# Fading the mLSTM state on ScalarE and adding only its diagonal blocks on VectorE

## The chip, the cores and the metric

One core of a Trainium2 chip runs the whole program. The metric is the device time of one execution in microseconds (us). Engines are named as in the profile: PE is TensorE, DVE is VectorE, ACT is ScalarE, POOL is GpSimd, SP is SyncE, whose queue (SPq) issues nearly all DMAs.

## The reference

Three layers follow each other; only the first is touched. It is an mLSTM over 2 batches, 8 heads, 768 time steps and a head width of 40:

```python
for t in range(S):
    m_new = np.maximum(f_gate[:, :, t] + m, i_gate[:, :, t])
    f_stab = np.exp(f_gate[:, :, t] + m - m_new)
    i_stab = np.exp(i_gate[:, :, t] - m_new)
    C = f_stab[..., None, None] * C + i_stab[..., None, None] * np.einsum('bhd,bhe->bhde', vt, kt)
    n = f_stab[..., None] * n + i_stab[..., None] * kt
    y_t = sigmoid(o_gate_t) * einsum('bhde,bhe->bhd', C, qt) / max(|n . qt|, 1)
```

The second layer is a spatially gated MLP, the third a channel mix, both with float32 results.

## The kernel before, in words

The 768 steps of a batch are cut into 6 chunks of 128, so there are 12 positions, taken in the order `SEQ` = 0, 6, 1, 7, 2, 8, ... (a chunk of batch 0, then the same chunk of batch 1). At a position the kernel computes the scores within the chunk (`scores`, `logd`), the contribution of earlier chunks through the state (`inter`), the state after the chunk (`state`, L478), the products with the values (`intra`), and the division (`normalise`), and transposes the result (`turn`) for the MLP.

The state of a batch is a tile `cn` of 120 rows by 8 x 41 columns. Heads go in groups of three (0 to 2, 3 to 5, 6 to 7): one matmul per group (L491) makes the keys of all the group's heads times the values of all of them, so of each 120 x 123 result in the PSUM tile `sp` only the three 40 x 41 blocks on the diagonal, a head with itself, are wanted. For a batch's first chunk ACT copies `sp` to `cn` (L512); for later ones DVE computes `cn * decay + sp` with one instruction for each group (`gather`, L500). In both cases POOL then multiplies `cn` by a 0/1 mask `bm_sb` (`blocks`, L505, two instructions) and clears the blocks off the diagonal. `bm_sb` is made once by ACT (L510) from a loaded tile `bm_raw`. The next reader of `cn` is `inter` (L527) of the same batch, two positions later. The last chunk of a batch makes no state, so there are ten state updates: two first ones and eight later ones.

The order of each engine's queue is fixed when the program is built, by a small planner. It keeps a clock for PE and a free time for DVE (`V`), ACT (`A`) and POOL (`P`). Work off PE is a `chain` of steps, each with an engine and a cost, which becomes ready 0.2 after the clock; a step follows the one before it by its cost plus `HOP` = 0.15. Whenever PE's clock moves (`beat`), `advance` issues the steps whose planned start lies before it, earliest start first; chains of weight splitting (`widen`, `wsp_half`) carry a handicap (`late`). Between the tasks of a position `fill(n, 1.0)` puts up to n matmuls of the MLP (`vp`, `up`) into PE's queue as long as their inputs' planned due time is within 1.0 of the clock. While the plan sees PE waiting with no filler ready, in the first eight positions, `heat` inserts matmuls on the identity (`wp`, L348). A changed cost in a chain can thus change the order in all four queues. `sp` holds one of six PSUM banks of the pool `psa` until the mark `("Cs", i)`.

Of the kernel before, what the change touches and what calls it, by code (L numbers as in the profile page):

```python
# [7 lines left out]
F32 = mybir.dt.float32  # L8
# [3 lines left out]
BF16 = mybir.dt.bfloat16  # L12
AF = mybir.ActivationFunctionType
ALU = mybir.AluOpType
# [3 lines left out]
def tile_mlstm_gmlp_channelmix(  # L18
# [25 lines left out]
    SEQ = [6 * b + c for c in range(6) for b in range(2)]  # L44
    P = 128
    H, D = 8, 40
    DA = D + 1
# [8 lines left out]
    GRP = ((0, 3), (3, 3), (6, 2))  # L56

    vec, act, pool, pe = nc.vector, nc.scalar, nc.gpsimd, nc.tensor
# [5 lines left out]
    at = tc.alloc_tile_pool(name="at", bufs=1, side="right")  # L64
# [88 lines left out]
    def beat(cost):  # L153
        clock[0] += cost
        advance(clock[0])
# [14 lines left out]
    def chain(key, *steps, ready=None):  # L170
        running.append(Chain(key, steps, clock[0] + 0.2 if ready is None else ready, 0.0))

    def finish(*keys, stall=True):
        for k in keys:
            while any(b[0] == k or b[0][0] == k for b in back):
                if not force_feed():
                    break
            for c in [c for c in running if c.has(k)]:
                while c in running and c.has(k):
                    advance(c.start(), skip=c)  # L180
                    if not c.open():
                        finish(split[0], stall=False)
                    if c in running and c.has(k):
                        issue(c)
        if stall:
            at_least(max([done.get(k, 0.0) for k in keys], default=0.0))
# [40 lines left out]
    def bank(pl, tag, name, *keys):  # L227
        own(tag, 6 if tag == "at" else 2, *keys)
        return pl.tile([P, 512], F32, tag=tag, name=name)
# [61 lines left out]
    def rows3(t, w):  # L291
# [8 lines left out]
    ig = gp.tile([16, S], F32, name="ig")  # L300
    f2, i2, ex_sb, pk_sb = (gp.tile([96, n], F32, name=nm)
                            for nm, n in (("f2", P), ("i2", P), ("ex_sb", 120), ("pk_sb", 6 * NCH)))
    bm_sb = at.tile([120, H * DA], BF16, name="bm_sb")
    mg = gp.tile([16, S + 1], F32, name="mg")
    ones = gp.tile([96, P], F32, name="ones")
    dec = at.tile([120, 6, NCH], F32, name="dec")
# [8 lines left out]
    def load_qk(i):  # L315
        b, c = divmod(i, NCH)
        t = at.tile([P, 2, 4, P], F32, tag="qk", name=f"qk{i}", bufs=2)
        for hh in range(2):
            e = load(t[64 * hh:64 * hh + D], qk[b, c, hh], 164)
        st["q", i], st["k", i] = t[:, 0], t[:, 1]  # L320
        st["at", i] = e
# [11 lines left out]
    def load_o(u):  # L333
        b, j = divmod(u, 2)
        o = at.tile([P, 3, DM], F32, tag="og", name=f"og{u}", bufs=3)
        load(o, o_tok[b, j], 480)
        st["o", u] = o
# [13 lines left out]
    for a in 'i f d o2 o0 q'.split():  # L351
        dict(f=lambda: sync.dma_start(out=fg, in_=f_gate), i=lambda: sync.dma_start(out=ig, in_=i_gate),
             d=lambda: sync.dma_start(out=id_sb, in_=ident), o=lambda: load_o(int(a[1])), q=lambda: load_qk(SEQ[0]))[a[0]]()
# [125 lines left out]
    def state(i):  # L479
        b, c = divmod(i, NCH)  # L480
        vt = st["vt", i]
        if c == NCH - 1:
            return
        wait(("kw", i))
        kw = st.pop(("kw", i))
        sp = bank(psa, "at", f"sp{i}", ("Cs", i))
        if c == 0:
            st["C", b] = at.tile([120, H * DA], F32, name=f"cn{b}")
        cn = st["C", b]
        for g, (h0, n) in enumerate(GRP):  # L490
            pe.matmul(sp[:n * D, h0 * DA:(h0 + n) * DA],  # L491
                      kw[:, h0:h0 + n, :].rearrange("p h d -> p (h d)"),
                      vt[:, h0:h0 + n, :].rearrange("p h d -> p (h d)"), start=True, stop=True)
        beat(0.57)
        parts = ((3 * D, slice(0, 6 * DA)), (2 * D, slice(6 * DA, 8 * DA)))

        def gather():
            for g, (h0, n) in enumerate(GRP):
                sl = slice(h0 * DA, (h0 + n) * DA)
                vec.scalar_tensor_tensor(out=cn[:n * D, sl], in0=cn[:n * D, sl], in1=sp[:n * D, sl],  # L500
                                         scalar=dec[:n * D, 3 * b + g, c:c + 1], op0=ALU.mult, op1=ALU.add)

        def blocks(eng, x):
            for n, sl in parts:
                eng.tensor_tensor(out=cn[:n, sl], in0=bm_sb[:n, sl], in1=x[:n, sl], op=ALU.mult)  # L505

        if c == 0:
            def fetch():
                if i == SEQ[0]:
                    act.copy(bm_sb, bm_raw)  # L510
                for n, sl in parts:
                    act.copy(cn[:n, sl], sp[:n, sl])  # L512

            chain(("C", i), ("A", 0.6, fetch, ("Cs", i)), ("P", 1.0, lambda: blocks(pool, cn)))
        else:
            finish(("dec", 0), stall=False)
            chain(("C", i), ("V", 0.75, gather, ("Cs", i)), ("P", 1.0, lambda: blocks(pool, cn)))

    def inter(i):
        b, c = divmod(i, NCH)  # L520
# [230 lines left out]
    def wait(*keys):  # L751
        while True:
            gap = eta(keys) - clock[0]
            if gap <= 0.02:
                break
            if fillers and eta(fillers[0][2]) <= clock[0] + 0.1:
                fill(1)
            elif warm[0] and gap > 0.2:
                heat(1)
                advance(clock[0])  # L760
            else:
                break
        finish(*keys)
# [26 lines left out]
    bm_raw = at.tile([120, H * DA], F32, tag="vr", name="bm_raw", bufs=2)  # L790
# [41 lines left out]
    def position(p):  # L832
# [20 lines left out]
        def st_():  # L853
            if p == 2:
                finish(("eg", "c"), ("dec", 0), stall=False)
                gp.release()
                lsp_.append(tc.alloc_tile_pool(name="lsp", bufs=1, side="left", reuse_waits="tile"))
                vec.tensor_scalar(out=omu_sb, in0=mu_sb, scalar1=-1.0, scalar2=1.0, op0=ALU.mult, op1=ALU.add)
            state(i)
# [64 lines left out]
    while todo:  # L924
        p = todo[0]["p"]
# [185 lines left out]
    for g in range(2 * B):  # L1111
# [8 lines left out]
        for j in range(3):  # L1120
            sl = slice(j * P, (j + 1) * P)
# [6 lines left out]
        for j in range(3):  # L1128
            sl = slice(j * P, (j + 1) * P)
# [120 lines left out]
```

## Time and profile before

| | |
|---|---|
| three runs | 332.76, 334.08, 334.0 us; median 334.0 |
| profiled execution | 334.12 us, span 332.4 us |
| mean granted PE clock | 0.937 of full speed |
| PE busy | 310.5 us (93%) |
| PE weight loads busy | 287.8 us (87%) |
| DVE busy | 230.0 us (69%) |
| ACT busy | 158.2 us (48%) |
| POOL busy | 157.0 us (47%) |

The profile is one execution. A busy time is the union of an engine's instructions; "idle before" names what ended a wait. The granted clock is a share of full speed, and has two levels, 0.5 (1.2 GHz) and 1.0 (2.4 GHz). The mLSTM takes the first 127 us or so of the span, its states the stretch from 20 to 111 us; the matmuls of the MLP's first layer fill PE beside it until 142 us.

### The profile page before, as it was taken

The page shows a single profiled execution, that of the slowest core. Times are in us where ns is not written, and L with a number is a line of the kernel's source. Part 1 is how long each engine was busy: PE and PEld are TensorE (multiplying, and loading weights), DVE is VectorE, ACT ScalarE, POOL GpSimd, SP SyncE. Part 2 cuts the span into 40 slices and gives each one's busy share as a digit, 9 for nine tenths or more (in the row PEclk, how much of TensorE's full clock was granted, in tenths as well). Part 3 has the DMA queues.
Part 4 walks back from the last instruction along what each step waited for, and adds up shares of the span by engine and source line. Part 5 has one row for each costly group of instructions (what it writes and reads, how often), then busy time and mean ns, then how long its engine had stood idle before and what let it go on. Part 6 is the DMA issues. An engine that isn't in the chain of part 4 may idle for free.

```text
span 332.4 us, 5459 instructions
## 1 busy us (share of the span) xinstructions
PE 310.5 (93%) x1985; PEld 287.8 (87%) x1985; DVE 230.0 (69%) x424; ACT 158.2 (48%) x316; POOL 157.0 (47%) x203
## 2 busy tenths in 40 slices
PE   5899996999999999999999999658999999999995
PEld 3586675898988988999999999547999999999995
DVE  6558599976877887776697956996655655654621
ACT  4552363238454344552345426348783753753620
POOL 4046267674878763783384660664501601601600
PEclk9656998799999999999999999965999999999999
DMA  6855651343543322356023320320001001001001
GB/s 182 270 140 173 221 152 63 94 151 100 166 117 100 113 63 65 98 167 210 2 80 127 106 78 14 109 78 0 0 2 60 3 20 39 2 20 41 0 20 41
DMA packets 12854, 28.97 MB, mean 87 GB/s; under 512 B 2099, under 2 KB 6187, under 8 KB 12827
## 3 DMA queue, kind: packets, MB, share of 16 engines
q1 hardware_dynamic: 12795, 28.56, 27.6%
q8 instruction: 16, 0.26, 0.3%
q14 instruction: 11, 0.09, 0.1%
q0 software_dynamic: 32, 0.07, 0.1%
HBM read 26.35 MB, written 1.97 MB: 85 GB/s over the span
## 4 chain that ended last, share of the span: by engine, by line
PE 76%; DVE 12%; ACT 3%; DMA 3%; issue 2%; POOL 2%; SPq 1%; DVEq 0%; POOLq 0%; ACTq 0%
PE spp L614 15%; PE vv L614 13%; PE kp L614 12%; PE vp L614 6%; PE wop L614 6%; PE up L614 5%; PE av L543 5%; PE rp L614 4%; DMA qk<-in_qk_dram 3%; PE sc L444 3%; PE wp L348 2%; PE ld L453 2%; DVE wbits L274 2%; DVE wbits L270 2%; PE sp L491 2%
## 5 line engine op out<-in xcount | busy, mean ns | idle before, releaser
L1103 POOL TENSOR_TENSOR sq<-sq 128x384 f32<-128x384 f32 x32 | 27.1, 852 | 60.9 <-ACT sq L1102 60.9
L614 PE MATMUL kp<-xk,wk 128*128 128x384 f32 x256 | 46.3, 338 | 4.6 <-DVE vs L1001 4.6
L614 PE MATMUL spp<-wsp,vn 128*128 128x384 f32 x288 | 50.4, 334 | 0.0
L614 PEld LDWEIGHTS spp<-wsp,vn 128*128 128x128 f32 x288 | 49.9, 188 | 0.0
L614 PEld LDWEIGHTS kp<-xk,wk 128*128 128x128 f32 x256 | 44.7, 189 | 5.2 <-DVE vs L1001 5.2
L614 PE MATMUL vv<-wv,k 128*128 128x320 f32 x288 | 42.9, 309 | 0.0
L614 PEld LDWEIGHTS vv<-wv,k 128*128 128x128 f32 x288 | 42.4, 188 | 0.0
L232 DVE TENSOR_TENSOR k<-sq,k 128x384 fp32r<-128x384 f32 x32 | 25.6, 801 | 21.7 <-ACT k L1104 21.7
L614 PE MATMUL up<-xg,w_u 128*128 128x256 f32 x192 | 32.5, 295 | 0.9 <-ACT u L696 0.6
L614 PE MATMUL vp<-w_v,xg 128*128 128x512 f32 x96 | 30.0, 428 | 2.0 <-ACT xg L605 1.2
L614 PE MATMUL wop<-gt,wo 128*128 128x384 f32 x128 | 27.4, 375 | 3.5 <-DVE vs L1001 2.5
L614 PEld LDWEIGHTS wop<-gt,wo 128*128 128x128 f32 x128 | 25.8, 216 | 4.9 <-ACT wv L285 3.0
L543 PEld LDWEIGHTS av<-kvq,dt 128*128 128x128 f32 x192 | 27.4, 215 | 0.8
L614 PEld LDWEIGHTS up<-xg,w_u 128*128 128x128 f32 x192 | 26.4, 190 | 1.8 <-ACT u L696 0.8
L1002 POOL TENSOR_TENSOR vs<-vs,u 128x384 f32<-128x384 f32 x16 | 20.5, 1279 | 13.7 <-DVE vs L1001 13.7
L543 PE MATMUL av<-kvq,dt 128*128 128x41 f32 x192 | 26.8, 294 | 0.0
L466 DVE TENSOR_TENSOR dt<-dt,sc 128x512 f32<-128x512 f32 x24 | 16.4, 682 | 11.2 <-ACT dt L463 9.4
L274 DVE SCALAR_TENSOR_TENSOR wbits<-wsq,wbits 128x320 int32<-128x320 int32 (+1 forms) x27 | 20.1, 748 | 4.2 <-ACT wsq L269 3.9
L1102 ACT ACTIVATE sq<-kp 128x384 f32<-128x384 f32 x32 | 15.4, 491 | 15.6 <-PE kp L614 15.6
L614 PEld LDWEIGHTS vp<-w_v,xg 128*128 128x128 f32 x96 | 17.9, 198 | 5.4 <-ACT xg L605 1.9
L463 ACT ACTIVATE dt<-ld 128x512 f32<-128x512 f32 x24 | 14.4, 600 | 17.0 <-PE ld L455 9.2
L1142 DVE TENSOR_TENSOR ob<-rs,vv 128x320 f32<-128x320 f32 x12 | 5.8, 487 | 21.3 <-PE vv L614 21.3
(160 smaller groups left out, 578.9 us busy)
## 6 DMA issues: line engine op xcount, KB each, us to landing
kvq<-in_kvq_dram SPq DMA_DIRECT2D x10, 516.0 KB
qk<-in_qk_dram SPq DMA_DIRECT2D x24, 160.0 KB
wraw<-in_w_k_dram SPq DMA_DIRECT2D x6, 512.0 KB
wraw<-in_w_v_dram SPq DMA_DIRECT2D x8, 320.0 KB
wraw<-in_w_sp_dram SPq DMA_DIRECT2D x12, 192.0 KB
og<-in_o_tok_dram SPq DMA_DIRECT2D x4, 480.0 KB
out_dram<-ob SPq DMA_DIRECT2D x12, 160.0 KB
w_inv<-in_w_in_dram SPq DMA_DIRECT2D x3, 512.0 KB
```

Source lines behind the costliest of these rows:

```text
L232: eng.tensor_tensor(out=out, in0=a, in1=b.bitcast(F32), op=ALU.subtract)
L270: vec.tensor_single_scalar(out=bits, in_=low_, scalar=29, op=ALU.logical_shift_right)
L274: vec.scalar_tensor_tensor(out=t["bits"], in0=t["sq"].bitcast(I32), scalar=3, in1=t["bits"], op0=ALU.logical_shift_left, op1=ALU.bitwise_or)
L348: pe.matmul(wp[:, :256], junk[:, :P], junk, start=True, stop=True)
L444: pe.matmul(st["sc", i, x][:, h * P:(h + 1) * P], k_[64 * x:64 * x + D, h, :], q_[64 * x:64 * x + D, h, :], start=True, stop=True)
L463: ("A", 0.48, lambda: act.activation(out=d2, in_=ld, func=AF.Exp), ("e", i, hh)),
L466: ("V", 0.6, lambda: vec.tensor_tensor(out=d2, in0=d2, in1=sc, op=ALU.mult)))
L543: pe.matmul(av[:, 4 * hh + h, :], A[:, h, :], vt[:, 4 * hh + h, :], start=True, stop=True)
L614: pe.matmul(out[0], l, x, start=j == 0, stop=j == len(prs) - 1)
L1002: ("P", 0.96, lambda: pool.tensor_tensor(out=vs, in0=vs, in1=ut[b][:, d, sl], op=ALU.mult)),
L1102: chain(("k2", g, f), ("A", 0.37, lambda: act.activation(out=sq, in_=ps, func=AF.Relu), ("kp", g, f)), ("P", 0.96, lambda: pool.tensor_ten ...
L1103: ("P", 0.96, lambda: pool.tensor_tensor(out=sq, in0=sq, in1=sq, op=ALU.mult)),
```

## The change

The state starts as zeros (one memset on POOL for each batch). For a later chunk ACT first multiplies `cn` by its decay, one instruction for each of the three groups (`fade`). DVE then adds from `sp` only the blocks on the diagonal (`gather`): instruction j takes the heads j, j+3, j+6 (a stride of three heads) and rows 0 to 40(j+1), and multiplies `sp` by column j of `bm_sb`, which is 1 in the 40 rows of the head and 0 above them. `bm_sb` becomes a tile of 120 x 3, one strided copy on ACT. POOL's multiplication by the mask goes. The planner's chain was DVE 0.75 (ACT 0.6 for a first chunk), then POOL 1.0; it is now ACT 0.75 (0.2 for a first chunk), then DVE 1.0, and the PSUM bank is given back after the DVE step as the second step of the chain, not the first.

```diff
-    bm_sb = at.tile([120, H * DA], BF16, name="bm_sb")
+    bm_sb = at.tile([120, 3], F32, name="bm_sb")
...
-        parts = ((3 * D, slice(0, 6 * DA)), (2 * D, slice(6 * DA, 8 * DA)))
+
+        s3, c3 = (t.rearrange("p (h d) -> p h d", h=H) for t in (sp[:, :H * DA], cn))
+
+        def fade():
+            if i == SEQ[0]:
+                act.copy(bm_sb, bm_raw[:, 0:3 * DA:DA])
+            if c > 0:
+                for g, (h0, n) in enumerate(GRP):
+                    sl = slice(h0 * DA, (h0 + n) * DA)
+                    act.activation(out=cn[:n * D, sl], in_=cn[:n * D, sl], func=AF.Copy, scale=dec[:n * D, 3 * b + g, c:c + 1])
 
         def gather():
-            for g, (h0, n) in enumerate(GRP):
-                sl = slice(h0 * DA, (h0 + n) * DA)
-                vec.scalar_tensor_tensor(out=cn[:n * D, sl], in0=cn[:n * D, sl], in1=sp[:n * D, sl],
-                                         scalar=dec[:n * D, 3 * b + g, c:c + 1], op0=ALU.mult, op1=ALU.add)
-
-        def blocks(eng, x):
-            for n, sl in parts:
-                eng.tensor_tensor(out=cn[:n, sl], in0=bm_sb[:n, sl], in1=x[:n, sl], op=ALU.mult)
+            for j, r in enumerate((D, 2 * D, 3 * D)):
+                vec.scalar_tensor_tensor(out=c3[:r, j:H:3], in0=s3[:r, j:H:3], in1=c3[:r, j:H:3],
+                                         scalar=bm_sb[:r, j:j + 1], op0=ALU.mult, op1=ALU.add)
 
         if c == 0:
-            def fetch():
-                if i == SEQ[0]:
-                    act.copy(bm_sb, bm_raw)
-                for n, sl in parts:
-                    act.copy(cn[:n, sl], sp[:n, sl])
-
-            chain(("C", i), ("A", 0.6, fetch, ("Cs", i)), ("P", 1.0, lambda: blocks(pool, cn)))
+            pool.memset(cn, 0.0)
         else:
             finish(("dec", 0), stall=False)
-            chain(("C", i), ("V", 0.75, gather, ("Cs", i)), ("P", 1.0, lambda: blocks(pool, cn)))
+        chain(("C", i), ("A", 0.75 if c else 0.2, fade), ("V", 1.0, gather, ("Cs", i)))
```

## Rows read from the trace of the kernel before

**Rows 1.** The page's first part: busy time, share and instructions by engine.
```profile
PE 310.5 (93%) x1985; PEld 287.8 (87%) x1985; DVE 230.0 (69%) x424; ACT 158.2 (48%) x316; POOL 157.0 (47%) x203
```
**Rows 2.** Stretches: length, PE, PEld, DVE, ACT, POOL busy, PE clock, DMA share, GB/s.
```profile
40.00:50.00 10.00, 9.21 (x75) 7.43 (x71) 9.67 (x23) 5.64 (x12) 6.77 (x9) 1.00 0.55 176
50.00:60.00 10.00, 7.31 (x36) 5.82 (x33) 9.38 (x19) 3.33 (x6) 8.26 (x11) 0.74 0.19 54
...
201.00:226.00 25.00, 17.25 (x84) 15.22 (x82) 23.15 (x40) 13.70 (x29) 10.49 (x10) 0.85 0.23 67
```
**Rows 3.** PE's waits from 37 to 142 us, the four longest: total, times, longest.
```profile
PE tp L591 <- DVE x L568: 1.5, 3, 0.8
PE vp L614 <- ACT xg L605: 1.2, 1, 1.2
PE tp L591 <- POOL x L571: 0.7, 1, 0.7
PE vp L614 <- DVE xg L232: 0.7, 1, 0.7
```
**Rows 4.** Stretches of 1 us around PE's waits, columns as in rows 2.
```profile
46.00:47.00 1.00, 0.31 (x1) 0.30 (x2) 0.94 (x4) 0.67 (x2) 1.00 (x2) 1.00 0.42 160
...
52.00:53.00 1.00, 0.27 (x2) 0.20 (x2) 1.00 (x3) 0.00 (x0) 0.74 (x2) 1.00 0.47 180
53.00:54.00 1.00, 0.29 (x3) 0.14 (x1) 0.55 (x2) 0.62 (x1) 1.00 (x3) 1.00 0.00 0
54.00:55.00 1.00, 0.53 (x2) 0.19 (x1) 1.00 (x3) 0.30 (x1) 1.00 (x2) 0.94 0.00 0
55.00:56.00 1.00, 0.25 (x1) 0.25 (x2) 1.00 (x4) 1.00 (x3) 1.00 (x2) 0.50 0.00 0
...
61.00:62.00 1.00, 1.00 (x14) 0.93 (x12) 1.00 (x1) 0.00 (x0) 1.00 (x1) 0.65 0.25 87
```
**Rows 5.** Groups by form: count, busy us, mean ns of one, idle before, releaser.
```profile
L505 POOL TENSOR_TENSOR cn<-bm_sb,cn 120x246 f32<-120x246 bf16 x10 | 8.4, 843 | 11.6 <-ACT cn L512 7.0 <-DVE cn L500 4.5
...
L505 POOL TENSOR_TENSOR cn<-bm_sb,cn 80x82 f32<-80x82 bf16 x10 | 4.7, 468 | 0.0
...
L1003 ACT CAST gt<-vs 128x384 fp32r<-128x384 f32 x16 | 8.2, 510 | 12.0 <-POOL vs L1002 12.0
...
L1039 ACT ACTIVATE tm<-x,omu_sb 128x384 f32<-128x384 f32 x24 | 13.9, 610 | 0.0
...
L512 ACT COPY cn<-sp 120x246 f32<-120x246 f32 x2 | 0.7, 365 | 2.7 <-PE sp L491 2.7
...
L384 ACT CAST Lxc<-f 96x128 fp32r<-96x128 f32 x1 | 0.3, 297 | 0.0
...
L500 DVE SCALAR_TENSOR_TENSOR cn<-cn,dec,sp 120x123 f32<-120x123 f32 x16 | 4.7, 334 | 0.0
...
L500 DVE SCALAR_TENSOR_TENSOR cn<-cn,dec,sp 80x82 f32<-80x82 f32 x8 | 2.3, 288 | 0.0
```
**Rows 6.** The tile wp: ns min/median/max, first and last start.
```profile
L348 PE MATMUL wp<-id_sb x61: 269/371/421, 3.6 to 38.9; 128*128 128x256 bf16 x61
```
**Rows 7.** DVE and POOL in order of time: start, us, instruction.
```profile
28.81 1.65 DVE L381 TENSOR_TENSOR i<-i,m 96x128 f32<-96x128 f32 x1
...
41.24 0.42 DVE L270 TENSOR_SCALAR wbits<-w_inu 128x512 int32<-128x512 int32 x1
...
47.08 1.28 POOL L232 TENSOR_TENSOR w_u<-wsq,w_u 128x512 fp32r<-128x512 f32 x1
...
47.59 1.05 DVE L270 TENSOR_SCALAR wbits<-w_inu 128x512 int32<-128x512 int32 x1
```
**Rows 8.** ACT in order of time, with the idle time before.
```profile
43.85 0.48 ACT L605 CAST xg<-tp 128x384 fp32r<-128x384 f32 x1 [0.79 <-PE tp L591]
...
53.22 0.62 ACT L285 CAST w_u<-wsq 128x512 fp32r<-128x512 f32 x1 [2.04 <-DVE wsq L278]
54.70 0.62 ACT L683 CAST vn<-vr 128x512 fp32r<-128x512 f32 x1 [0.86 <-DVE vr L681]
55.23 0.47 ACT L605 CAST xg<-tp 128x384 fp32r<-128x384 f32 x1
```

## The prediction

> **What bounds the kernel now.** I read the busy shares first, then the stretches, then PE's waits, then the queues around the longest of them. PE is busy for 310.5 us of a span of 332.4 [rows 1]. So an edit that touches no matmul can gain only where PE stands still or runs at the lower clock. The stretches say where that is: PE is nearly full everywhere except between 40 and 60 us, where DVE is the full engine (9.67 and 9.38 of 10), and between 201 and 226 us [rows 2]. The second place lies 90 us behind the last state update and is DVE splitting weights; I leave it as it is. The states are updated in the first place and up to 111 us. From 37 to 142 us PE's four longest waits come to 1.5 + 1.2 + 0.7 + 0.7 = 4.1 us [rows 3]. Between 52 and 56 us PE is busy for only 0.27, 0.29, 0.53 and 0.25 us of each microsecond, and behind that the granted clock falls to 0.50, its lower level of 1.2 GHz, and is back in the row of 61 to 62; the single poor microsecond at 46, between full ones, cost no clock [rows 4]. What the fall costs: 0.06 + 6 x 0.5 + 0.35 = 3.4 us of full-speed time, less the half of the 0.75 us in which PE stood idle anyway at 55, makes 3.0 us [rows 4]. So 4.1 us of waits and 3.0 us of clock are all that the change can win near its own place, and the same mechanism is what it can lose.
>
> **The change part by part.**
>
> *POOL* loses 8.4 + 4.7 = 13.1 us in 20 instructions [rows 5]. It gains two memsets; the trace has none of their shape, so each costs between nothing and the 0.843 of the removed instruction of like size, and they lie where POOL now waits 7.0 us for ACT's first copies [rows 5]. None of PE's long waits is for the mask's output: what releases them is a transposition's input or `xg` [rows 3]. So the 13.1 us are worth nothing directly. Indirectly they could free DVE, which waits for POOL in places: the same DVE instruction takes 0.42 us at 41.24 and 1.05 at 47.59, while POOL's 1.28 us subtraction runs [rows 7]. I compared each DVE instruction beside the ten masks with its undisturbed twin: about 1.9 us are lost in all, most of it in one of 1.65 us at 28.81 [rows 7], none of it in front of a wait in [rows 3]. I take nothing, with 0 and -1.9 us as the ends.
>
> The Trainium skill (SBUF — State Buffer, section "SBUF: two separate sides") says VectorE and GpSimd lock one shared port pair for whole instructions, and that a VectorE instruction with two SBUF inputs is among those that block. By it every removed mask could free DVE for its whole length, at most 13.1 us as an estimate, and the sum would be that much lower. The 1.05 us at 47.59 agrees that such blocking exists; the 1.9 us found beside the masks says that these rarely collide.
>
> *ACT* gains eight fades. The trace shows no such instruction. A cast of 96x128 takes 297 ns; a scale taken from a tile costs 610 - 510 = 100 ns more at 128x384 [rows 5]. So 0.40 us for 123 columns, about 0.36 for 82; together 1.16, or about 0.96 in a row, since neighbours overlap by 0.1. The ends are 3 x 0.297 = 0.9 and 3 x 0.61 = 1.8 us. It loses the two copies at first chunks (0.365 and a smaller one) and most of one cast. A fade reads only `cn` and the decays, not the new matmul, so it can run while PE still makes `sp`. ACT has the room: it is busy 5.64 and 3.33 us of the two tight stretches [rows 2], and stands idle 0.79 us at 43, just about one fade, and 2.04 us before 53.22 [rows 8]. Cost nothing, as long as it goes into those gaps. Without them, it stands before the next cast of `xg` with its whole 0.96 us (the slower rival below).
>
> *DVE* keeps three instructions per state, of the same widths: 2 x 0.334 + 0.288 = 0.96 us in place of the same sum [rows 5]. The strided heads are not in the trace; the ends are no change and double. I take no change, since a mean of 334 ns for 123 columns is mostly fixed cost. New are the gathers of the two first chunks, 2 x 0.96 = 1.9 us, between 19 and 29 us, where PE is at the half clock and its queue carries the `wp` matmuls, 61 by 38.9 us [rows 6]; the next real dependence there is on DMA, so nothing. By the costs in the chains the first chunk's gather delays DVE's plan by 1.0 and lightens POOL's by as much, which about cancels in the due time that decides the number of `wp`; the ends are -7 and +7 of them, at 0.1 to 0.2 us, within +-1.4 us.
>
> *PE* and *DMA* get no new work. SP's queue keeps its order, and the mask's load stays. The bank of `sp` is held up to one fade longer; no wait of PE in [rows 3] is for a bank, so nothing, and 0.96 us if that were wrong at one place.
>
> *The order.* This is where I expect the effect. A gather becomes ready 0.75 + 0.15 later in the plan than before and is costed 0.25 higher. So weight splitting and score products that stood behind it on DVE go ahead of it. At the state at 45 us this lets the split that feeds `w_u` start one gather, about 0.8 us, earlier; POOL's 1.28 us at 47.08 then ends before the DVE instruction at 47.59, which gets back its 1.05 - 0.42 = 0.6 us [rows 7]. I take 0.5 for the two transposition waits behind it. At the state at 54.6 us the low half of `xg` gets a later due time (0.25 to 1.15 by the costs). In PE's queue a single `vp` matmul is put there as a filler ahead of eight `av`, and PE waits 1.2 us for the `xg` cast of 55.23 with the `av` ready behind it [rows 3, 8]. A filler must be due within 1.0; with the later due time it drops behind the `av`, and the 1.2 us goes. What is late next is then that same `xg` with the `av` already done, some tenths.
>
> *Sum.* -0.5 - 1.2 = -1.7 us on the profiled 334.12 us (span 332.4 and 1.7 around it), which lies 0.1 above the median of 334.0. I predict 332.3 us.
>
> **The rivals.**
>
> *The clock stays up.* If those 1.7 us of work move into the poor microseconds 52 to 56, PE's clock may not fall there: another -3.0, 329.3 us. For it: the one poor microsecond at 46 did not bring the clock down. Against: two waits of 0.7 for the transposition remain in the same place.
>
> *Nothing moves.* The plan slides but PE's queue keeps its order, or what is won at 52 to 56 is waited for again at the next `xg`: 334.0, give or take 0.5.
>
> *Slower: a fade in front of `xg`.* ACT runs in order. At 54.70 to 55.7 it casts `vn` and directly behind it `xg`, for which PE waits [rows 8]. If the plan puts the fade of 0.96 us between the two, PE's wait grows by that; it decides from the point where a fade starts after the `vn` cast rather than in the 2.04 us before 53.22. The gather then waits too, and behind it on DVE the score product and the low half of `xg`: 0.96 + 0.96 for two steps in a row. With one such place 334.0 + 1.9 = 335.9, and if the longer gap keeps the clock down half as long again or lowers it at a second place (1.5 to 3.0 us), up to 338.9. I give 336.5. For it: DVE is the full engine there [rows 2], so every wait of a gather is passed on. Against: the fade is ready early, since it waits only for the `inter` matmuls before it.
>
> *It does not do what it says.* Should the strided gather cost double, DVE gets 0.96 us more at each of ten states, two of them in the tight stretch: +1.9 us, in with the slower case.
>
> **How the numbers follow.** The forecast 0.36, with its own range 331.3 to 333.3; clock up 0.24; nothing moves 0.18; slower 0.22. About 0.5% of 334, 1.7 us, is what a measurement of this kernel tells from no change, and the three runs shown lie 1.3 us apart. The forecast sits on that bound, so half of it and all of the clock case make faster: 0.18 + 0.24 = 0.42, and 0.02 from runs below in the case where nothing moves. Slower is 0.22, same the remaining 0.34. The range reaches from the middle of the clock case's spread, 328.8, to just past the middle of the slower one, 336.8.
>
> **What would show it.** Right: L505 gone, three ACT instructions of 0.35 to 0.40 us in ACT's gaps, three DVE instructions at the old length; PE's wait of 1.2 us on `xg` gone and fewer poor microseconds between 52 and 56; the stretches behind 142 us as long as before. The clock rival: no row at 0.50 between 54 and 62. Wrong: a fade between `vn` and `xg` casts, longer gathers, other numbers of `wp`, or a difference that arises behind 201 us, for which I have made no case.

## The result and the profile after

| | before | after |
|---|---|---|
| median of the runs beside each other | 334.04 us (332.76 to 335.58, 4 runs) | 329.49 us (327.45 to 331.01, 4 runs) |
| profiled execution | 334.12 us, span 332.4 | 327.45 us, span 325.7 |
| mean granted PE clock in it | 0.937 | 0.974 |

The ratio is 0.9888 with an interval of [0.9841, 0.9936]: faster by 0.6 to 1.6%. The forecast was 332.3 us, its range 328.8 to 336.8. Two more times the unchanged new kernel ran beside the kernel before (below), with 0.9868 [0.9811, 0.9925] and 0.9952 [0.9902, 1.0002]. A ratio leaves out the slow runs, those more than 1.5% above the fastest of the same program (three of the six and four of the twelve in these two), while the means named below take every run, one stray run of over 1.6 ms excepted. By means the new kernel stands at 331.6 us (22 runs) and the kernel before at 333.0 (78 runs), 0.4% apart; in the three measurements the difference of the means is 4.8, 1.7 and 0.3 us. The profiled execution after is the fastest of its four, so its 6.7 us are more than the change is worth.

In the program after, lines behind the state are two lower (L614 is now L612, L591 is L589, L605 is L603, L683 is L681). The first part of its page, against [rows 1]:

```profile
PE 302.4 (93%) x1982; PEld 281.5 (86%) x1982; DVE 224.3 (69%) x430; ACT 163.2 (50%) x336; POOL 145.6 (45%) x185
```

PE is busy for 8.1 us less with only three matmuls less: what changed is mostly how long its matmuls took, at a mean granted clock of 0.974 in place of 0.937. The new instructions, from the view of the tile `cn` (count, ns min/median/max, first and last start), against [rows 5]:

```profile
L508 DVE SCALAR_TENSOR_TENSOR cn<-sp,bm_sb,cn x30: 282/326/331, 19.5 to 100.6; 40x123 f32<-40x123 f32 x10, 80x123 f32<-80x123 f32 x10, 120x82 f32<-120x82 f32 x10
L504 ACT ACTIVATE cn<-cn,dec x24: 347/386/412, 39.1 to 99.4; 120x123 f32<-120x123 f32 x16, 80x82 f32<-80x82 f32 x8
L512 POOL MEMSET cn<- x2: 366/367/368, 14.2 to 25.8; 120x328 f32 x2
```

PE's waits from 33 to 142 us, against [rows 3]: the transposition `tp` waits for less, the wait for `xg` stands at 1.4, and two waits of `spp`, the MLP's matmul with the split weight `w_sp`, are new.

```profile
PE vp L612 <- ACT xg L603: 1.4, 1, 1.4
PE spp L612 <- POOL vn L232: 0.9, 1, 0.9
...
PE spp L612 <- ACT vn L681: 0.6, 1, 0.6
PE tp L589 <- POOL x L569: 0.3, 1, 0.3
```

What the chart of PE shows around the first place, before and then after (start, us, instruction, idle before in brackets):

```profile
52.73 0.41 PE L591 MATMUL tp<-id_sb,x 128*128 128x128 f32 x2 [0.76 <-DVE x L568]
53.85 0.33 PE L591 MATMUL tp<-id_sb,x 128*128 128x128 f32 x1 [0.71 <-POOL x L571]
...
55.75 0.80 PE L614 MATMUL vp<-w_v,xg 128*128 128x512 f32 x1 [1.22 <-ACT xg L605]
56.34 1.77 PE L543 MATMUL av<-kvq,dt 128*128 128x41 f32 x8
```

```profile
47.63 0.42 PE L589 MATMUL tp<-id_sb,x 128*128 128x128 f32 x2
48.38 0.33 PE L589 MATMUL tp<-id_sb,x 128*128 128x128 f32 x1 [0.33 <-POOL x L569]
...
48.90 0.98 PE L541 MATMUL av<-kvq,dt 128*128 128x41 f32 x8
...
51.26 1.58 PE L612 MATMUL vp<-w_v,xg 128*128 128x512 f32 x5 [1.37 <-ACT xg L603]
```

Both transpositions' waits shrink, 0.76 + 0.71 to 0.33, and the eight `av` stand ahead of the wait for `xg`. The same stretch by time, against [rows 2] and [rows 4] (length, busy of PE, PEld, DVE, ACT, POOL, granted clock, DMA share, GB/s):

```profile
40.00:50.00 10.00, 8.77 (x67) 7.15 (x66) 9.05 (x20) 4.54 (x11) 5.93 (x8) 1.00 0.47 140
50.00:60.00 10.00, 8.74 (x58) 7.36 (x58) 9.03 (x24) 5.47 (x12) 7.97 (x10) 0.83 0.23 73
...
50.00:51.00 1.00, 0.00 (x0) 0.00 (x0) 1.00 (x4) 0.79 (x2) 0.10 (x1) 1.00 0.32 25
...
55.00:56.00 1.00, 1.00 (x4) 0.71 (x4) 0.97 (x3) 0.76 (x2) 0.36 (x2) 0.50 0.00 0
56.00:57.00 1.00, 1.00 (x8) 0.90 (x6) 0.58 (x1) 0.72 (x2) 1.00 (x1) 0.76 0.01 2
```

One microsecond without any matmul is left (50 to 51), and the clock still falls behind it, though for a shorter time here.

A ledger by five marks in PE's queue (start in us: the first `tp`, the first and third `ip`, the last `tp`, the first `wop`, which is the matmul with `w_out`) shows where profiled executions differ. The three columns to the right are experiments explained below: the old and the new program, each with twelve more `wp`, and the version that came out best.

| | before | after | old, more `wp` | new, more `wp` | best |
|---|---|---|---|---|---|
| first `tp` | 31.19 | 26.87 | 28.04 | 26.29 | 25.72 |
| first `ip` | 41.07 | 37.17 | 37.91 | 36.75 | 36.04 |
| third `ip` | 63.32 | 56.41 | 61.47 | 57.69 | 53.73 |
| last `tp` | 127.93 | 119.11 | 127.66 | 121.83 | 117.80 |
| first `wop` | 166.97 | 160.89 | 166.69 | 165.21 | 157.82 |
| end of span | 332.4 | 325.7 | 331.8 | 330.0 | 323.1 |

Of the 8.8 us by which the profile after leads at the last `tp`, 4.3 are there at the first one; 2.7 are lost again before the first `wop`; from there both take 165 us. Three questions follow. Are the first 4.3 us the change's? Does the gain at 41 to 63 us come from the order or from the work? Why is part given back?

### The profile page after: what moved, and what is told of

The parts are those of the page before. It is cut to its first block, busy times and chain, and to the rows that moved or that the text cites. A ratio compares the mean times of both kernels' runs of the same rounds, so it can differ in the third digit from the quotient of the medians.

```text
span 325.7 us, 5486 instructions
## 1 busy us (share of the span) xinstructions
PE 302.4 (93%) x1982; PEld 281.5 (86%) x1982; DVE 224.3 (69%) x430; ACT 163.2 (50%) x336; POOL 145.6 (45%) x185
## 4 chain that ended last, share of the span: by engine, by line
PE 74%; DVE 10%; ACT 5%; POOL 4%; DMA 3%; issue 2%; SPq 1%; DVEq 0%; ACTq 0%; POOLq 0%
PE spp L612 14%; PE vv L612 13%; PE kp L612 12%; PE vp L612 6%; PE wop L612 5%; PE up L612 5%; PE av L541 5%; PE rp L612 4%; PE sc L444 3%; DMA w_inv<-in_w_in_dram 2%; PE ld L453 2%; DVE wbits L274 2%; PE wp L348 2%; PE ip L525 2%; PE sp L491 1%
## 5 line engine op out<-in xcount | busy, mean ns | idle before, releaser
L612 PE MATMUL spp<-wsp,vn 128*128 128x384 f32 x288 | 51.0, 335 | 1.5 <-POOL vn L232 0.9
L612 PEld LDWEIGHTS spp<-wsp,vn 128*128 128x128 f32 x288 | 49.8, 188 | 2.2 <-POOL vn L232 1.2
L612 PE MATMUL kp<-xk,wk 128*128 128x384 f32 x256 | 45.9, 336 | 4.6 <-DVE vs L999 4.6
L612 PEld LDWEIGHTS kp<-xk,wk 128*128 128x128 f32 x256 | 44.4, 188 | 5.2 <-DVE vs L999 5.2
L612 PE MATMUL vv<-wv,k 128*128 128x320 f32 x288 | 43.4, 310 | 0.1
L612 PEld LDWEIGHTS vv<-wv,k 128*128 128x128 f32 x288 | 42.4, 188 | 0.6 <-DVE k L232 0.3
L612 PE MATMUL vp<-w_v,xg 128*128 128x512 f32 x96 | 29.3, 422 | 2.3 <-ACT xg L603 1.4
L612 PE MATMUL up<-xg,w_u 128*128 128x256 f32 x192 | 31.2, 293 | 0.0
L612 PE MATMUL wop<-gt,wo 128*128 128x384 f32 x128 | 25.7, 358 | 4.5 <-DVE vs L999 2.9
L612 PEld LDWEIGHTS wop<-gt,wo 128*128 128x128 f32 x128 | 24.1, 203 | 5.7 <-ACT wv L285 3.2
L612 PEld LDWEIGHTS up<-xg,w_u 128*128 128x128 f32 x192 | 26.2, 190 | 0.5
L541 PEld LDWEIGHTS av<-kvq,dt 128*128 128x128 f32 x192 | 25.7, 203 | 0.7
L541 PE MATMUL av<-kvq,dt 128*128 128x41 f32 x192 | 25.3, 284 | 0.0
L274 DVE SCALAR_TENSOR_TENSOR wbits<-wsq,wbits 128x320 int32<-128x320 int32 (+1 forms) x27 | 21.3, 793 | 2.5 <-ACT wsq L269 2.1
L612 PEld LDWEIGHTS vp<-w_v,xg 128*128 128x128 f32 x96 | 17.5, 194 | 5.8 <-DVE xg L232 1.5
```

Of the source, the lines that this page charges most:

```text
L274: vec.scalar_tensor_tensor(out=t["bits"], in0=t["sq"].bitcast(I32), scalar=3, in1=t["bits"], op0=ALU.logical_shift_left, op1=ALU.bitwise_or)
L541: pe.matmul(av[:, 4 * hh + h, :], A[:, h, :], vt[:, 4 * hh + h, :], start=True, stop=True)
L612: pe.matmul(out[0], l, x, start=j == 0, stop=j == len(prs) - 1)
```

## The experiments

My theory for the second question was the prediction's: order, not work. The rival was that taking work from POOL frees VectorE, which it blocks in places. The first four programs ran beside each other. Without an edit, the program after:

> The changed kernel once more, as the yardstick. Order theory (the planner's new costs re-order the queues): 0.985 to 0.992 of the kernel before. Clock theory (the 4.3 us that the first profile of the changed kernel is ahead at 27 us stem from a clock that happened to stay up from 10 to 19 us): the median comes nearer to the kernel before, 0.990 to 0.997, and the profile shows the clock at 0.50 from 11 us on as before.

Measured: median 331.21 us (326.03 to 335.43, 6 runs), ratio 0.9868 [0.9811, 0.9925]. The profiled run had a span of 330.6 us, 4.9 more than the first profile of the same program. The kernel before spreads far less: the standard deviation over 23 runs beside it is 1.1 us, over these six 3.0. By the ratio the first theory holds, by means (331.13 against 332.85, or 0.9948) the second. The profile decides neither: the clock does fall at 10 us, but it is back at 17 and not at 30, and the first `ip` comes at 37.43.

Old instructions, new costs in the plan (`"D"` is an engine that the plan counts as free):

```diff
+        def fetch():
+            if i == SEQ[0]:
+                act.copy(bm_sb, bm_raw)
+        def take():
+            if c > 0:
+                return gather()
+            for n, sl in parts:
+                act.copy(cn[:n, sl], sp[:n, sl])
...
-            chain(("C", i), ("V", 0.75, gather, ("Cs", i)), ("P", 1.0, lambda: blocks(pool, cn)))
+        chain(("C", i), ("A", 0.75 if c else 0.2, fetch), ("V", 1.0, take, ("Cs", i)), ("D", 0.0, lambda: blocks(pool, cn)))
```

> The old instructions (decay and sum on VectorE, mask on GpSimd, first chunk copied by ScalarE) in the order that the planner makes of the new costs; PE's queue is that of the changed kernel. Order theory: as the changed kernel, 0.985 to 0.992 of the kernel before. Work theory (GpSimd's 13.1 us of masks gone is what helps): as the kernel before, 0.997 to 1.003. Both: between them.

Measured: 332.51 us (330.45 to 337.87, 12 runs), 0.9996 [0.9966, 1.0026]. PE's queue has the order of the program after, and from the first to the third `ip` it takes 19.1 us, as that one does (19.2; before 22.3). Yet nothing of it reaches the end. The number is the work theory's here, and the order theory's in the next experiment, so neither holds alone. In the profile (of its slowest run) the clock is at 0.59 between 70 and 80 us, where no other profile has a fall. Ahead of that fall PE waits for `x`:

```profile
71.32 0.63 PE L593 MATMUL tp<-id_sb,x 128*128 128x128 f32 x3 [1.39 <-DVE x L570]
```

That `x` is late because a DVE instruction ahead of it (`dn`, L559, at 67.52) takes 2.71 us while POOL works through three instructions that stand behind a mask of 1.15 us (65.14). In the program after, with no mask there, the same instruction takes 1.02 us and PE does not wait. So in this order the masks are in the way.

New instructions, old costs:

```diff
-        chain(("C", i), ("A", 0.75 if c else 0.2, fade), ("V", 1.0, gather, ("Cs", i)))
+        def both():
+            fade()
+            gather()
+        chain(("C", i), ("V", 0.75, both, ("Cs", i)) if c else ("A", 0.6, both, ("Cs", i)), ("P", 1.0, lambda: None))
```

> The new instructions (fade on ScalarE, strided gather on VectorE, no mask) in the order that the planner makes of the old costs; PE's queue is that of the kernel before. Order theory: as the kernel before, 0.997 to 1.005 (the fade now stands directly in front of its gather). Work theory: 0.985 to 0.992.

Measured: 331.58 us (330.27 to 334.83, 12 runs), 0.9978 [0.9948, 1.0009]. Its PE waits where the kernel before does, though POOL has no masks:

```profile
49.90 0.41 PE L593 MATMUL tp<-id_sb,x 128*128 128x128 f32 x2 [0.73 <-DVE x L570]
51.01 0.33 PE L593 MATMUL tp<-id_sb,x 128*128 128x128 f32 x1 [0.70 <-POOL x L573]
...
52.91 0.79 PE L616 MATMUL vp<-w_v,xg 128*128 128x512 f32 x1 [1.04 <-ACT xg L607]
```

So the waits belong to the order, and taking the masks away alone is worth 0.2%, within its interval of nothing. By means it is 0.8 us (332.09 against 332.85), where the program after beside it has 1.7 (331.13); with six runs that spread by 3 us the times do not tell these two apart.

The traces do, for one stretch. This program and a later one (the program after with more `wp`, first of two measurements) have the same work and the same clock from 30 to 200 us, 1.00 except for 0.57 at 50 to 60 and 0.92 at 60 to 70, but the two orders (start in us):

| | new work, old order | new work, new order |
|---|---|---|
| first `ip` | 38.28 | 37.56 |
| third `ip` | 61.71 | 58.49 |
| last `tp` | 126.23 | 122.64 |
| first `wop` | 165.26 | 164.44 |
| end of span | 330.1 | 329.4 |

From the first to the third `ip` the new order takes 20.9 us for 23.4; from the first `ip` to the first `wop` both take 127 (126.98 and 126.88). The gain at 41 to 63 us is the order's, and with the clock alike all of it is given back before the end.

The program after, with POOL's masks put back behind the gather, unknown to the plan (they multiply by ones and zeros what is masked already; ACT also makes the mask again, once, with one copy):

```diff
+        def masks():
+            for n, sl in ((3 * D, slice(0, 6 * DA)), (2 * D, slice(6 * DA, 8 * DA))):
+                pool.tensor_tensor(out=cn[:n, sl], in0=bm_old[:n, sl], in1=cn[:n, sl], op=ALU.mult)
-        chain(..., ("V", 1.0, gather, ("Cs", i)))
+        chain(..., ("V", 1.0, gather, ("Cs", i)), ("D", 0.0, masks))
```

> The changed kernel with the old masks put back on GpSimd behind each gather, unknown to the planner (they multiply by 1 or clear zeros); the rest of every queue as in the changed kernel. Order theory: as the changed kernel to within 0.3%. Work theory: back to the kernel before, 0.997 to 1.003.

Measured: 336.67 us (336.14 to 340.22, 6 runs), 1.013 [1.0088, 1.0172]; its mean is 4.5 us above the kernel before and 5.7 above that of the program after. That is beyond what either theory allowed. In the new order the masks are not free: the transposition now waits for POOL, and the instruction `dn` takes 2.71 us here too.

```profile
PE tp L595 <- POOL x L575: 1.3, 2, 1.0
```

The next four ran beside each other. The program after, unchanged:

> The changed kernel a third time, beside the next three on one chip, for the spread over runs: time against mean granted clock. Clock theory: its runs lie on one falling line with those of the kernel before (about 141 us for each 1.0 of clock), at most 1 us apart at the same clock, and its mean over all runs is 1 to 3 us below. Order theory: 2 us or more below at the same clock.

Measured: 333.24 us (328.83 to 338.99, 12 runs), 0.9952 [0.9902, 1.0002]; by means 0.3 us below the kernel before. Straight lines of time over mean granted clock, through all 22 runs of the new program and the 74 of the kernel before for which the clock is on record, lie 0.3 us apart at a clock of 0.95 (332.14 and 332.48); at 0.94 the new program is 0.5 above, at 0.96 it is 1.2 below. Its mean clock is higher, 0.953 against 0.946. So the clock theory fits better, though its 1 to 3 us of means are 0.3 here: most of the difference goes with the clock.

The split of `w_out`, which stands in ACT's queue ahead of the last `vr` and `vn`, moved behind the last MLP matmuls:

```diff
-    for j in range(4):
-        widen("w_o", ...)
     closing.append(0)
     fill(len(fillers) + len(later))
+    for j in range(4):
+        widen("w_o", ...)
```

> The changed kernel with the splitting of w_out planned only behind the last filler matmuls; PE's queue is the same. In the changed kernel a cast of w_out stands in ScalarE's queue for 4.78 us and keeps back the last vr and vn steps, and PE waits 0.65 and 0.87 us at 137 to 139. Order theory (the new order gains 2.4 us at 40 to 60 and gives 2.2 us back at 133 to 139): the stretch from the last transposition to the first wop matmul shortens from 41.9 by 2 us, and the time by about that, 0.6% below the changed kernel. Rival: something else is late next there, no gain.

Measured: 338.21 us (331.19 to 342.38, 12 runs), 1.0026 [0.997, 1.0082]. The rival happened: the waits for `vn` are gone, and `spp` waits longer for splits of `w_sp`, which the moved work now overtook. From the last `tp` to the first `wop` it takes 48.7 us (after: 41.8), and by means the program is 5.1 us slower than the unchanged one beside it (337.70 against 332.64), which the ratio hides.

```profile
PE spp L612 <- DVE wsp L232: 2.1, 2, 1.8
PE spp L612 <- ACT wsp L731: 1.4, 2, 0.7
```

Twelve more `wp` ahead of the first scores, `heat(34)` for `heat(22)`:

> The changed kernel with 34 in place of 22 matmuls on the identity ahead of the first scores, so that PE does not stand idle at 8 to 9 us; nothing else differs. Clock theory (whether the clock falls at 10 us decides 3 to 4 us at 27 us): the clock is 1.00 to 17 us in the profile, the mean clock rises by 0.01 to 0.02 over the changed kernel and the median falls by 2 to 3 us, with less spread. Rival (the first 30 us are bound by DMA and VectorE, not by PE's clock): no change in time.

Measured: 330.57 us (326.17 to 331.99, 6 runs), 0.9842 [0.9773, 0.991]; by means 2.8 us below the unchanged program beside it (329.80). The clock is at 1.00 up to 20 us, as expected. Both edits together:

> The last two edits together on the changed kernel. If both theories hold, they add: 4 to 5 us below the changed kernel, 0.975 to 0.983 of the kernel before. If the clock's part is chance that the matmuls do not touch, only 0.6% below the changed kernel.

Measured: 334.14 us (333.17 to 340.83, 12 runs), 1.0027 [0.9992, 1.0062]. By means it is 2.6 us above the unchanged program, about the sum of what the two edits did alone (5.1 up and 2.8 down); the first had no gain to add.

The last four ran beside each other. The order of the matmuls left over for the end, `vp` before `up`:

```diff
-    fill(len(fillers) + len(later))
+    fillers.extend(later)
+    later.clear()
+    k = len(fillers) % 8
+    groups = [fillers[j:j + 8] for j in range(k, len(fillers), 8)]
+    groups.sort(key=lambda g: -g[0][1])
+    fillers[k:] = sum(groups, [])
+    fill(len(fillers))
```

> The changed kernel with one difference: of the matmuls that are left for the stretch behind the last transposition, the eight vp of the last position go ahead of the up matmuls instead of between them. Theory (what the change wins at 37 to 58 us it partly gives back at 133 to 139, because the last vn is finished too late): the last vp ends about 3.4 us earlier, vn with it, both waits of spp for vn (0.65 and 0.87 us) go, the distance from the last transposition to the first wop matmul falls from about 42 to about 40.4 us, and the mean of all runs is 1 to 1.5 us below that of the changed kernel. Rival (another step of the same queues comes last, as when the w_out split was moved): the waits turn into waits for a part of w_sp, the distance stays at 41.5 or more, and the time stays where it was.

Measured: 326.08 us (324.8 to 328.37, 6 runs), 0.9805 [0.9756, 0.9853], the best of all; the standard deviation of its runs is 1.2 us. PE goes from the `up` matmuls to `spp` without a wait, and from the last `tp` to the first `wop` it takes 40.0 us (after: 41.8):

```profile
124.86 7.83 PE L612 MATMUL up<-xg,w_u 128*128 128x256 f32 x64
132.54 0.69 PE L612 MATMUL spp<-wsp,vn 128*128 128x384 f32 x3
```

The same with twelve more `wp`:

> The same with twelve more wp matmuls before the first scores (heat(34) for heat(22)). Theory: the two gains add, since they lie 110 us apart: about 1.5 us below the kernel with twelve more wp alone. Rival: no lower than that kernel, as when the other rearrangement was put together with it (334.1 against 330.6).

Measured: 328.28 us (325.84 to 329.55, 6 runs), 0.9856 [0.9811, 0.9901]. By means that is 2.7 us below the kernel with twelve more `wp` alone, run beside it (328.05 against 330.75; 1.8 without the two longest of that kernel's twelve runs), but not below the rearrangement alone: the two don't add.

The kernel before with the twelve `wp`:

> The kernel before, unchanged but for the same twelve wp matmuls. Theory (the clock before 30 us is a matter of how PE is fed there and not of this change): the kernel before gains as well, its clock is at 1.00 for part of 10 to 30 us, and the mean falls by 1 to 3 us. Rival (the early clock comes with the change's own work): the clock stays at 0.50 from 10 to 30 us and the time does not fall, or rises by the 12 x 0.1 to 0.2 us of the matmuls.

Measured: 333.18 us (330.79 to 333.97, 12 runs), 1.0003 [0.9971, 1.0035]. Half of each theory: the early clock came up, the time did not fall.

And the program after with them, once more:

> The changed kernel with twelve more wp matmuls, again, beside the kernel before with the same twelve. Theory: 329 to 331 us again, and 0.5 to 2.5 us below the kernel before with the twelve, which is what the change is worth when both start alike. Rival (the first time was chance): 332 to 334.

Measured: 330.22 us (327.44 to 335.67, 12 runs), 0.9914 [0.988, 0.9949]; by means 2.05 us below the old program with the twelve (330.75 against 332.80).

## Why the prediction came out, point by point

**What the masks were worth.** Priced at nothing, and the old order with the new work (0.9978) agrees within its interval. Blocking between the two engines does show at single instructions: the one that took 1.05 us at 47.59, begun while POOL's subtraction ran [rows 7], takes 0.41 in the first profile after, where it begins just ahead of POOL's next instruction (41.01 against 41.15).

```profile
41.01 0.41 DVE L270 TENSOR_SCALAR wbits<-w_inu 128x512 int32<-128x512 int32 x1
```

But no mask is the other party in either, and the short time is not the rule: in seven of the nine profiles of the new program, as it is or with later edits but no masks, POOL begins first and the instruction takes 0.94 or 0.95 us. In the second profile of the unchanged program PE's wait for the low half of `xg` is 1.3 us by it, where the first has 0.8. The Trainium skill (SBUF — State Buffer, section "SBUF: two separate sides") says that VectorE and GpSimd exclude each other on a shared port pair; these rows agree. "Nothing" holds for the old order alone: masks that the new order doesn't know cost 5.7 us, and they are what the old work in the new order runs into.

**The prices.** A fade of three instructions was put at 0.96 us and took 0.93; the strided gather was to cost no more, and three in a row take 0.79 us as the old three did (at 41.34 after, at 44.90 before); a memset, put below 0.843, took 0.367. The rival of the double price falls.

**The two steps of the sum.** -0.5 us at the transpositions was too little: 1.47 became 0.33. It also came by another path than the one named. The split that was to start earlier comes later (its last DVE step, L278, stands 4.6 us behind the first `ip` before and 6.9 after). What shrank is the work on DVE between `nn` and the `x` of the transposition: two splitting steps and the statistics of `vr` before (0.68, 1.03 and 0.68 us), one splitting step of 1.33 us after. -1.2 us at `xg` was named as a wait that goes with "some tenths" left; the wait stayed (1.22 and 1.37) and the work behind it went ahead: eight `av`, 0.98 us at the full clock. The step predicted the right move and the wrong trace of it. Together, from the first to the third `ip` the pair with twelve more `wp` and the same fall of the clock shows 23.56 against 20.94 us; four `up` matmuls (0.47 us) have moved behind it, so 2.2 us against the 1.7 of the sum. The pair with the new work in both orders shows 23.43 against 20.93, 2.0 without these four.

**The slower rival.** It did not come. At the place that it named, no fade stands between `vn` and `xg`; the fade lies in a gap 2 us ahead of the pair:

```profile
48.29 0.93 ACT L504 ACTIVATE cn<-cn,dec 120x123 f32<-120x123 f32 x3
50.21 0.62 ACT L681 CAST vn<-vr 128x512 fp32r<-128x512 f32 x1 [0.99 <-DVE vr L679]
50.73 0.47 ACT L603 CAST xg<-tp 128x384 fp32r<-128x384 f32 x1
```

At two other states a fade does stand there (39.06 and 98.80 us, both behind a `vn`). The first went into the gap that the prediction had found at 43 us, now nearly four us earlier, and PE's wait behind it is 0.78 us in this profile where it was 0.69 before.

**The clock rival.** In all five profiles of the new program, as it is or with more `wp`, it fell all the same (0.83, 0.55, 0.66, 0.57 and 0.53 over 50 to 60 us). In one of the best version, whose queues are the same up to 118 us, it stayed up, and from the first to the third `ip` it took 17.7 us (20.9 for the new program with more `wp`). So this case exists, as a matter of the execution, not of the change alone:

```profile
50.00:60.00 10.00, 9.88 (x84) 8.53 (x85) 8.93 (x23) 4.37 (x11) 8.88 (x12) 1.00 0.26 87
```

**What I did not see: what is given back.** I wrote that the stretches behind 142 us would be as long as before, and looked no further than the waits near the states. The new order puts three `vp` more behind the last `tp` and an ACT cast of `w_out` ahead of a `vr`. By the trace that cast waits for the last `vp` (its target is a page from a pool of twelve; that it takes one that `w_v` held is my reading of the program and not shown), and everything behind it in ACT's queue waits too. ACT after:

```profile
124.59 0.62 ACT L681 CAST vn<-vr 128x512 fp32r<-128x512 f32 x1 [0.83 <-DVE vr L679]
129.99 0.46 ACT L285 CAST wo<-wsq 128x320 fp32r<-128x320 f32 x1 [4.78 <-PE vp L612]
130.36 0.59 ACT L675 ACTIVATE vr<-vp 128x512 f32<-128x512 f32 x1
...
136.60 0.61 ACT L681 CAST vn<-vr 128x512 fp32r<-128x512 f32 x1
```

Before, a `vr` was taken ahead of the same cast, which stood for 1.32 us only:

```profile
135.16 0.60 ACT L677 ACTIVATE vr<-vp 128x512 f32<-128x512 f32 x1 [1.39 <-POOL vn L232]
...
138.14 0.46 ACT L285 CAST wo<-wsq 128x320 fp32r<-128x320 f32 x1 [1.32 <-PE vp L614]
```

PE then stands for 0.65 and 0.87 us after:

```profile
137.27 0.62 PE L612 MATMUL spp<-wsp,vn 128*128 128x384 f32 x2 [0.65 <-ACT vn L681]
138.75 1.50 PE L612 MATMUL spp<-wsp,vn 128*128 128x384 f32 x7 [0.87 <-POOL vn L232]
```

From the last `tp` to the first `wop` 39.0 us became 41.8. Three more `vp` are 0.7 of it, so 2 us are given back, about what was won. In some executions there is more. The second run of the same program has the same waits, and then the clock falls too; over 140 to 150 it stood at 0.83, another 1.7 us. In the first profile of it there was no fall.

```profile
141.00:142.00 1.00, 0.19 (x2) 0.00 (x0) 0.00 (x0) 0.92 (x3) 1.00 (x2) 1.00 0.18 28
...
144.00:145.00 1.00, 1.00 (x5) 1.00 (x4) 0.14 (x1) 1.00 (x3) 0.50 (x1) 0.50 0.03 12
```

Taking this wait away by the order of the last `vp` gave 1.8 to 2.7 us beside its twin. In profiles with the same clock falls it is 1.4: with twelve more `wp`, the first `ip` comes at 37.57 and 37.56 us and the first `wop` at 163.01 in place of 164.44. The runs lie closer together too, which would fit a fall that is gone: neither profile with this order has one at 140 to 150 us, and two of the five of the new program, as it is or with more `wp`, do. Moving the cast itself did not help, since it only changed which late work `spp` waits for.

**The first 4.3 us.** In the profile before, the clock is at 0.53 and 0.50 from 10 to 30 us. With twelve more `wp` the old and the new program look alike there, and the lead at the first `ip` shrinks from 3.9 to 1.2 us:

```profile
10.00:20.00 10.00, 10.00 (x55) 6.67 (x53) 5.89 (x10) 4.66 (x10) 0.72 (x1) 0.53 0.87 285
20.00:30.00 10.00, 10.00 (x47) 8.14 (x47) 6.85 (x12) 4.43 (x11) 8.04 (x9) 0.50 0.25 58
```

```profile
10.00:20.00 10.00, 9.23 (x78) 6.77 (x76) 6.28 (x11) 5.50 (x13) 1.51 (x2) 0.99 0.86 282
20.00:30.00 10.00, 9.24 (x56) 6.59 (x57) 9.96 (x14) 3.89 (x10) 7.84 (x9) 0.67 0.22 58
```

```profile
10.00:20.00 10.00, 9.15 (x77) 6.61 (x74) 6.50 (x13) 5.51 (x12) 2.02 (x3) 0.99 0.85 287
20.00:30.00 10.00, 9.49 (x60) 7.16 (x60) 9.66 (x21) 3.21 (x8) 5.20 (x6) 0.67 0.21 55
```

(The kernel before, then the old and the new program with more `wp`.) So about 2.7 of the 3.9 us are the clock of that one execution. The program with the masks put back agrees: its clock is at 0.50 from 10 to 30 us as well, and its first `ip` comes at 40.29, where the unchanged program has it at 37.17 to 37.43 in three profiles. Whether it is chance alone is open. The three profiles with so long a fall are the three with masks on POOL and 22 early `wp`, but no mask has started before 20.4 us, when other executions had the full clock back. The forecast had allowed 1.4 us for another number of `wp`; 58 in place of 61 is inside that.

**What it adds up to.** With the clock alike at the start, the change is worth 2.05 us by means (330.75 against 332.80; 2.95 without the two longest runs of the new program). The profiles of that pair come to 1.8: 1.2 up to the first `ip`; 4.7 from there to the last `tp`, of which 0.7 is `vp` moved behind it; 4.4 lost up to the first `wop`, made of that 0.7, waits of 1.5, a clock at 0.83 for 10 us (1.7), and 0.5 that I can't place; 0.3 won behind it. But in that pair the old program also has the lower clock at 60 to 70 us (0.79 against 0.96), another 1.7 us, so the two falls cancel. What is left with the clock alike is mostly the lead at the first `ip`, 1.2 us here and 0.7 in the pair of the two orders; three `wp` less are 0.3 to 0.6 of it at the prediction's 0.1 to 0.2 us each. From the first `ip` to the first `wop` the two pairs are 0.3 and 0.1 us apart.

So the forecast of -1.7 us is right in the place and near the size of the two steps, and wrong in holding that nothing else moves: what the new order does behind 118 us returns that gain. That the whole came out near the forecast is in part luck, for most of what remains goes with the granted clock, which the sum had left as it was and which only the clock rival moved. What stays open is why the mean clock of the new program is higher (0.953 against 0.946 over all runs), whether shorter waits keep it up or something else, and how much of the 2.05 us another set of runs would keep: the three ratios of the unchanged program reach from 0.9868 to 0.9952. The old work in the new order was profiled once, in its slowest run, so what the collision with the masks costs in its other runs is open too. And the best version leads the program after by 5.5 us of means, of which the waits and the clock behind them explain about 2 to 3.7; these two were not run beside each other.

## What to carry to other kernels

When an edit changes costs that a planner reads, price the order and the work apart: give the old work the new costs and the new work the old ones. Here neither alone gave a gain clear of noise, and the new order lost time as soon as the masks stood in it. Follow a moved order to the end of the stage: what is pulled ahead at one place may put a blocked instruction in front of another engine's queue 90 us later, and that instruction's own wait does not look like PE's. And one profile can carry several microseconds of clock that the change did not make: compare pairs whose clock falls at the same place. Such a pair showed here that a gain of 2.5 us at one place was worth nothing at the end.

## What the runs showed of the hardware

The same program, unchanged, ran between 326.0 and 339.0 us. Its four clock falls (within 10 to 30, 50 to 65, 140 to 150 and 200 to 235 us) differ in length from one execution to the next, and the one at 140 to 150 is missing in two of its three profiles. The kernel before and the new one issue the same matmuls up to about 15 us; in profiles where the clock fell at about 10 us it was back at 17 us in one of the new program and at 31 us in the one of the kernel before. More matmuls early kept the clock at 1.00 up to 20 us in both programs, but in the old one it was lower later (0.53 at 50 to 60 and 0.79 at 60 to 70 us, against 0.74 and 0.91), so its time did not move. A VectorE instruction that takes 0.17 us at its shortest (`dn`) took 2.71 us in both programs with masks in the new order, while GpSimd worked through three instructions. Another (`wbits`, L270) took 0.41 us where it began before a GpSimd instruction that waited for a DMA, and 0.94 or 0.95 where that one had begun first: an unchanged program can differ by half a microsecond through the order in which two engines begin.
